# W2 issued behind W1 with a wait in the q/k queue, and fp16 chunk bounds for the second halves of the first batch

## The chip, the cores and the metric

The kernel runs on one core of one Trainium2 chip. The metric is the device time of one execution in microseconds (us). TensorE is called PE here, VectorE DVE, ScalarE ACT, GpSimd POOL and SyncE SP. SP issues most DMAs and computes nothing; POOL issues the loads of v, W1 and W2 and also computes.

## What is computed

Sparse attention over chunks of keys, followed by a layer norm and a two-layer MLP with a residual. There are 4 batches, 8 heads, 768 positions and 64 values per head, all fp32 in and out.

```python
k_min, k_max = min and max of k over each chunk of 32 keys      # 24 chunks
ub = sum_d max(q * k_min, q * k_max)                            # bound of each chunk
ub = where(chunk is not in the future, ub, -1e9)
top = the 6 chunks with the largest bound, for each query
scores = q @ k.T / 8, kept where the key's chunk is in top and the key is not in the future
x = softmax(scores) @ v, heads side by side                     # (4, 768, 512)
xn = (x - mean) / sqrt(var + 1e-6) * g_ln
out = x + relu(xn @ w_ch1) @ w_ch2                              # 512 -> 2048 -> 512
```

## The kernel before

A group is one batch and one pair of heads: 16 groups, four per batch. The 768 positions are six tiles of 128; a half is three tiles. Batch 0 (groups 0 to 3) is worked through by halves: first halves of all four groups, then the second halves. Its units are called (g, i), with i = 0 or 1. Groups 4 to 15 are worked through whole.

The steps of one unit, in the code's names:

- `load_qk`: four DMAs on SP's queue bring k and q of a half. `load_v`: v on POOL's queue, with a change of type to fp16.
- `turn`: PE transposes k or q (fp32) into PSUM.
- `k_bound`: DVE takes min and max over each chunk, into `kc`.
- `k_diag`: builds a block matrix `BD` from the bounds for both heads. For groups from 4 on, POOL also splits it into high and low fp16 parts in `BH`.
- `q_copy`: in batch 0 ACT makes fp32 relu(-q) and relu(q), `q32` and `r32`; from group 4 on it makes a high fp16 part of q, and DVE the low part; `q_relu` makes the same two for relu(q).
- `bounds`: PE computes the chunk bounds. In batch 0 one bf16 matmul writes the causal mask into PSUM and two fp32 matmuls per tile add the bounds; from group 4 on there are four fp16 matmuls per tile of 96 columns, high and low parts side by side.
- `select`: DVE finds the sixth largest bound with `max` and writes the mask `MN`. From group 4 on it first adds the two column parts and the causal mask, `causf`.
- `mask_t`, `mask_ring`: PE transposes the mask, DVE copies it beside q in the score tiles `QA` and `QB`. `k_copy` fills `KA` and `KB`; from group 4 on by DMAs on SP's queue.
- `scores`, `diag`, `values`, `normalise`: scores on PE, exp on ACT, the diagonal's mask on POOL, the product with v on PE, the division on DVE into x.
- `stats`, `centre`, `rstd`, `x_t`, `mlp1`, `mlp2`: the layer norm and the MLP of half a batch (b, r), all with fp16 weights. `mlp1` takes two blocks of 128 hidden columns at a time, W1 in four pieces; `mlp2(b, r, i, j)` takes four of the sixteen hidden blocks (kt 4j to 4j + 3) of output tile i, and W2 comes in four pieces j by the same kt. After the last, DVE scales, adds x and SP stores the tile.

The order is written out by hand. Every step is put into a list with a time (`at`, and the list `begin` for the start); `MOVED` shifts single steps; the list is sorted by time and then executed, each engine's instructions in that order, which for the start is also made fixed. PE, DVE, ACT and POOL each work through their queue in order, so a waiting instruction holds all behind it. The loads of the start stand in the table `loads`:

```python
        4: [(load_v, 1, 1), (load_v, 2, 1), (load_qk, 4, 0)],
        5: [(w2_load, 0, 0), (w2_load, 1, 0), (load_v, 3, 1), (load_qk, 4, 1)],
        6: [(w2_load, 2, 1), (w2_load, 3, 1)],
```

`w1_load` and `w2_load` first copy one element of a group's `kc` into the piece, on POOL: that makes the transfer wait until this group's `k_bound` is through. Both queues' DMAs are also limited in number: a DMA takes one of eight semaphores in turn and waits until the DMA that had it before has landed.

Of the kernel before, what the change touches and what calls it, by code (L numbers as in the profile page):

```python
# [9 lines left out]
ACTF = mybir.ActivationFunctionType  # L10
ALU = mybir.AluOpType
# [8 lines left out]
def kernel(  # L20
# [21 lines left out]
    NR = 2  # L42
# [44 lines left out]
    RT = const.tile([P, S], F16, name="RT", tag="RT")  # L87
    tiny = const.tile([1, 1], F32, name="tiny", tag="tiny")
# [75 lines left out]
    def w2_load(j, g):  # L164
        nc.gpsimd.tensor_copy(w2b[0:1, 4 * j, 0:1], st[g]["kc"][0:1, 0, NCH // 2:NCH // 2 + 1])
        nc.gpsimd.dma_start(w2b[:, 4 * j:4 * j + 4, :], w2_r[:, 4 * j:4 * j + 4, :])

# [59 lines left out]

    def q_copy(g, i):
        pst = st[g]["qn", i]
        if g < HP:  # L230
            u = P if i == 0 else 0
            for e, (nm, sign) in enumerate((("q32", -1.0), ("r32", 1.0))):
                st[g][nm] = prp.tile([P, TR * P], F32, name=nm, tag=nm)
                nc.scalar.activation(st[g][nm][:, u:], pst[:, u:], ACTF.Relu, scale=sign)
            c = cols(g, i)
            nc.scalar.activation(QA[g % NK][0:64, c], pst[0:64, :], ACTF.Copy, scale=QS)
            nc.scalar.activation(QB[g % NK][64:P, c], pst[64:P, :], ACTF.Copy, scale=QS)
            return
# [44 lines left out]
    def k_diag(g, i=None):  # L283
# [4 lines left out]
        e, eng = (0, nc.vector) if g < HP else (1, nc.gpsimd)  # L288
        if g >= HP:
            eng.tensor_tensor(kc[:, 1], kc[:, 1], kc[:, 0], ALU.subtract)  # L290
# [4 lines left out]
        if g >= HP:  # L295
            bh = BH[g % NB]
            nc.gpsimd.tensor_copy(bh[:, :, 0], bd)
            nc.gpsimd.tensor_tensor(bh[:, :, 1], bd, bh[:, :, 0], ALU.subtract)

    def bounds(g, s, i=None, idle=0):  # L300
        p = st[g]
        a, z, n = chosen(g, i)
        if g < HP:
# [16 lines left out]
        else:  # L320
# [3 lines left out]
            o = p["ub"][:, s - 1].rearrange("p l h c -> p (l h c)")  # L324
# [6 lines left out]
    def select(g, i=None):  # L331
# [4 lines left out]
        if g >= HP:  # L336
            ubt = smp.tile([P, NT - 1, 2, NCH], F32, name="ubt", tag="ubt", bufs=1)
            ubm = smp.tile([P, NT - 1, 2, NCH], F32, name="ubm", tag="ubm")
            nc.vector.tensor_tensor(ubt, ub[:, :, 1], causf, ALU.add)
            nc.vector.tensor_tensor(ubm, ub[:, :, 0], ubt, ALU.add)  # L340
            ub = ubm
# [176 lines left out]
    def mlp2(b, r, i, j):  # L518
# [4 lines left out]
        for kt in range(4 * j, 4 * j + 4):  # L523
            nc.tensor.matmul(  # L524
                yp, h["hT"][:, kt, i * P:(i + 1) * P], w2b[:, kt, :],
                start=(kt == 0), stop=(kt == KT2 - 1),
            )
        if j == 3:
            ot = outp.tile([P, DM], F32, name="ot", tag="ot")
            nc.vector.scalar_tensor_tensor(  # L530
                ot, yp, h["rstd"][:, i:i + 1], xh(b, r)[:, i].rearrange("p h d -> p (h d)"),
# [3 lines left out]
            nc.sync.dma_start(out[b, s * P:(s + 1) * P, :], ot)  # L535
# [11 lines left out]
        4: [(load_v, 1, 1), (load_v, 2, 1), (load_qk, 4, 0)],  # L547
        5: [(w2_load, 0, 0), (w2_load, 1, 0), (load_v, 3, 1), (load_qk, 4, 1)],
        6: [(w2_load, 2, 1), (w2_load, 3, 1)],
        8: [(load_v, 4), (load_qk, 5, 0)],  # L550
# [111 lines left out]
    for b in range(B):  # L662
# [14 lines left out]
        if b == 0:  # L677
# [13 lines left out]
            (): -0.04, (0, 1): -0.009, (0, 2): -0.025, (1,): 0.008, (1, 1): 0.017, (1, 2): 0.017,  # L691
            (2,): 0, (2, 4): 0.006, (2, 5): 0.028, (3,): 0, (3, 1): 0.013, (3, 2): 0.013,
            (4,): -0.048, (5,): 0.008, (5, 5): 0.016, (6,): 0.004, (7,): -0.067, (7, 1): -0.07,
            (8,): -0.436, (9,): -0.025, (9, 5): -0.02, (11,): -0.044, (12,): -0.311, (13,): -0.144,
            (14,): -0.138, (14, 5): -0.134, (15,): -0.21, (15, 4): -0.176, (15, 5): 0,
        },
        "centre": {
            (): 0.008, (0,): -0.017, (0, 1): 0, (0, 1, 0): -0.017, (1,): 0, (1, 0, 2): 0.089,
            (1, 1): 0.033, (1, 1, 1): 0.026,
        },  # L700
        "diag": {
            (): -0.046, (0, 0): 0.016, (0, 1): 0.001, (1, 0): 0.012, (1, 1): -0.067, (2,): 0.003,
            (3, 0): -0.003, (3, 1): 0, (4,): -0.056, (6, 0): -0.044, (6, 1): -0.066, (7, 0): -0.178,
            (7, 1): -0.097, (8, 0): -0.399, (8, 1): -0.6, (9, 0): -0.066, (9, 1): -0.069, (11, 0): 0,
            (11, 1): -0.054, (12, 0): -0.04, (12, 1): 0, (13, 0): -0.146, (13, 1): -0.078,
            (14, 0): 0.003, (14, 1): 0, (15, 0): -0.621,
        },
        "k_bound": {
            (0,): -0.011, (1,): -0.011, (2,): -0.009, (3,): -0.018, (4, 0): 0.007, (4, 1): 0.027,
            (5, 1): 0.022, (6, 0): 0.002, (6, 1): 0.107, (7,): -0.058, (8, 0): -0.331,  # L710
            (8, 1): -0.396, (9, 0): 0.002, (9, 1): 0.065, (11, 0): -0.008, (11, 1): 0.025,
            (12, 0): -0.017, (12, 1): -0.015, (13,): -0.032, (14,): 0.028,
        },
        "k_copy": {
            (0,): -0.004, (1, 0): 0.161, (1, 1): 0.063, (2,): 0.006, (3, 0): -0.011, (3, 1): 0.054,
            (4,): 0.024, (5, 0): 0.511, (5, 1): 0.42, (6,): 0.038, (7, 0): -0.032, (9, 1): 0.023,
            (10,): 0.034, (11, 1): 0.026, (12, 0): 0.938, (12, 1): 0.253, (13, 0): 0.002,
            (13, 1): 0.073, (14,): 0.046, (15,): 0.034,
        },
        "k_diag": {  # L720
            (1,): 0.041, (2, 0): 0.13, (3, 0): 0.033, (3, 1): 0.01, (4,): -0.002, (6,): 0.002,
            (7,): -0.058, (8,): -0.331, (9,): -0.138, (10,): -0.023, (11,): 0.02, (12,): 0.006,
            (13,): -0.032, (14,): -0.108, (15,): -0.076,
        },
        "load_qk": {
            (): -0.438, (0, 0): 0.085, (0, 1): -0.538, (1, 0): 0.034, (1, 1): -0.331, (2, 0): 0,
            (2, 1): -0.329, (3, 0): 0.16, (3, 1): -0.169, (4, 0): -0.33, (4, 1): -0.667,
            (5, 0): -0.543, (5, 1): -1.259, (6, 0): 0.011, (6, 1): -0.111, (7, 0): 0.064,
            (7, 1): 0.002, (8, 0): -0.299, (8, 1): -0.593, (10, 0): 0.015, (10, 1): -0.002,
            (11, 0): -0.01, (11, 1): -0.012, (12, 0): 0.082, (12, 1): 0.004, (13, 0): 0.11,  # L730
            (13, 1): 0.159, (14,): 0.026, (15, 0): 0.317, (15, 1): 0.334,
        },
        "load_v": {
            (2,): -0.087, (3, 0): -0.13, (3, 1): -0.568, (4,): -0.551, (5,): -0.547, (6,): -0.163,
            (7,): 0.215, (8,): -0.124, (9,): 0.342, (12,): 0.279, (13,): 0.241, (14,): 0.301,
            (15,): 0.238,
        },
        "mask_ring": {
            (): 0.017, (0, 0): 0.021, (0, 1): 0, (1, 0): 0.036, (1, 1): -0.009, (2, 0): 0.023,
            (2, 1): 0, (4,): 0.064, (5,): 0.074, (6,): 0.076, (7,): 0.016, (8,): -0.257, (9,): 0.076,  # L740
            (10,): 0.209, (11,): 0.066, (12,): 0.08, (13,): 0.102, (14,): 0.139, (15,): 0.093,
        },
        "mask_t": {
            (): -0.004, (0,): 0, (1, 0): -0.019, (1, 1): -0.002, (2,): 0.002, (4,): -0.016,
            (5,): -0.068, (7,): -0.064, (8,): -0.337, (10,): -0.001, (11,): -0.014, (12,): 0.002,
            (13,): -0.082, (14,): 0, (15,): -0.006,
# [144 lines left out]
```

## Time and profile before

| | |
|---|---|
| median of 3 runs | 302.92 us (302.92 to 303.49) |
| profiled execution | 303.4 us, span 301.4 us, PE clock granted 0.997 |
| DMA moved | 31.41 MB, mean 104 GB/s |
| MLP matmuls on PE, L512 and L524 | 94.3 and 95.9 us of records |
| exp on ACT, L417 | 86.2 us |
| `bounds` in fp32, L316 | 48 + 32 records in batch 0, 15.0 us |
| `bounds` in fp16, L326 | 240 matmuls, 23.1 us |

The span starts with the first instruction and ends with the last. Busy times of PE are sums of records that overlap, because matmuls are pipelined; the distance between starts tells what a matmul costs. An fp32 matmul leaves two records. Most of the DMA traffic falls in the first 80 us.

```profile
GB/s 131 208 210 198 180 199 196 164 193 204 149 135 187 124 72 165 110 143 148 88 132 62 78 46 2 41 49 90 35 37 0 37 37 35 35 37 35 70 37 71
```

Each number is one fortieth of the span, 7.5 us.

### The profile page before, as it was taken

The page shows a single profiled execution, that of the slowest core. Times are in us where ns is not written, and L with a number is a line of the kernel's source. Part 1 is how long each engine was busy: PE and PEld are TensorE (multiplying, and loading weights), DVE is VectorE, ACT ScalarE, POOL GpSimd, SP SyncE. Part 2 cuts the span into 40 slices and gives each one's busy share as a digit, 9 for nine tenths or more (in the row PEclk, how much of TensorE's full clock was granted, in tenths as well). Part 3 has the DMA queues.
Part 4 walks back from the last instruction along what each step waited for, and adds up shares of the span by engine and source line. Part 5 has one row for each costly group of instructions (what it writes and reads, how often), then busy time and mean ns, then how long its engine had stood idle before and what let it go on. Part 6 is the DMA issues. An engine that isn't in the chain of part 4 may idle for free.

```text
span 301.4 us, 7194 instructions
## 1 busy us (share of the span) xinstructions
PE 288.2 (96%) x2753; PEld 195.4 (65%) x2753; DVE 190.8 (63%) x654; ACT 183.5 (61%) x274; POOL 91.1 (30%) x162
## 2 busy tenths in 40 slices
PE   7887998999999999999999999999999999999993
PEld 3874766765777676777767667766666555555541
DVE  7888655679998788999577768577262282011011
ACT  3983997664788667778665674848368524423310
POOL 9559383152444412733230411223021120000000
PEclk9999999999999999999999999999999999999998
DMA  7999999999659649679572210113010110010111
GB/s 131 208 210 198 180 199 196 164 193 204 149 135 187 124 72 165 110 143 148 88 132 62 78 46 2 41 49 90 35 37 0 37 37 35 35 37 35 70 37 71
DMA packets 90226, 31.41 MB, mean 104 GB/s; under 512 B 78416, under 2 KB 87120, under 8 KB 90192
## 3 DMA queue, kind: packets, MB, share of 16 engines
q1 hardware_dynamic: 60416, 23.61, 33.8%
q0 software_dynamic: 29248, 7.34, 24.8%
q8 instruction: 22, 0.36, 0.5%
q14 instruction: 12, 0.10, 0.1%
q10 hardware_dynamic: 528, 0.00, 0.1%
HBM read 27.27 MB, written 6.29 MB: 111 GB/s over the span
## 4 chain that ended last, share of the span: by engine, by line
PE 75%; DMA 8%; POOL 7%; issue 4%; DVE 4%; ACT 1%; POOLq 0%; ACTq 0%
PE yp L524 24%; PE mm L512 24%; PE mm L411 10%; PE sm L437 6%; PE tr L223 4%; DMA w2b<-in_moe_w_ch_dram 4%; DMA w1b<-in_moe_w_ch_dram 4%; PE ub L326 3%; POOL va L214 2%; PE trh L497 1%; POOL pt L424 1%; PE trh L354 1%; DVE xc L482 1%; ACT pt L417 1%; POOL rstd L491 1%
## 5 line engine op out<-in xcount | busy, mean ns | idle before, releaser
L417 ACT ACTIVATE pt<-mm 128x1024 f16<-128x1024 f32 (+1 forms) x96 | 86.2, 918 | 25.7 <-PE mm L411 25.3
L524 PE MATMUL yp<-w2b,hT 128*128 128x512 f16 x384 | 95.9, 379 | 1.5 <-DMA w2b<-in_moe_w_ch_dram 1.5
L512 PE MATMUL mm<-xT,w1b 128*128 128x384 f16 x512 | 94.3, 326 | 0.0
L516 ACT ACTIVATE hT<-mm 128x768 f16<-128x768 f32 x64 | 51.9, 813 | 49.1 <-PE mm L512 48.8
L512 PEld LDWEIGHTS <-w1b 128*128 128x128 f16 x512 | 48.9, 98 | 29.9 <-issue 0.2
L524 PEld LDWEIGHTS <-hT 128*128 128x128 f16 x384 | 36.4, 98 | 31.8
L424 POOL TENSOR_SCALAR_AFFINE_SELECT pt<-pt 128x768 f16<-128x768 f16 x32 | 28.8, 899 | 89.1 <-ACT pt L417 89.1
L530 DVE SCALAR_TENSOR_TENSOR ot<-yp,rstd,x 128x512 f32<-128x512 f32 x24 | 17.9, 746 | 45.9 <-PE yp L524 45.9
L411 PE MATMUL mm<-QA,KA 128*128 128x128 f16 (+2 forms) x224 | 34.5, 245 | 1.0 <-ACT hT L516 0.5
L411 PE MATMUL mm<-QB,KB 128*128 128x128 f16 (+2 forms) x224 | 34.2, 246 | 0.0
L437 PEld LDWEIGHTS <-pt 128*128 128x128 f16 x672 | 24.6, 98 | 5.6 <-POOL pt L424 1.8
L437 PE MATMUL sm<-va,pt 128*128 128x65 f16 x672 | 26.5, 193 | 1.4 <-POOL pt L424 1.3
L411 PEld LDWEIGHTS <-KA 128*128 128x128 f16 x224 | 17.9, 99 | 8.1 <-issue 2.3
L471 DVE BATCH_NORM_STATS2 bst<-x 128x6 f32<-128x128 f32 x96 | 21.9, 282 | 0.8
L268 DVE TENSOR_REDUCE kc<-tr 128x12 f32<-128x384 f32 x32 | 17.6, 549 | 6.6 <-PE tr L223 4.9
L411 PEld LDWEIGHTS <-KB 128*128 128x128 f16 x224 | 18.0, 98 | 3.5 <-issue 0.8
L446 DVE RECIPROCAL rden<-sm 128x6 f32<-128x6 f32 x32 | 6.1, 191 | 19.7 <-PE sm L437 19.6
L447 DVE TENSOR_TENSOR x<-sm,rden 128x384 f32<-128x384 f32 x32 | 17.8, 557 | 1.0
L223 PE MATMUL tr<-ident_f,qn 128*128 128x128 f32 x96 | 16.2, 278 | 1.3 <-DMA qn<-in_q_dram 1.3
L269 DVE TENSOR_REDUCE kc<-tr 128x12 f32<-128x384 f32 x32 | 17.5, 547 | 0.0
L279 ACT CAST kh<-tr 128x384 f16<-128x384 f32 x24 | 11.6, 484 | 9.2 <-DMA KB<-kh 3.2
L223 PE MATMUL tr<-ident_f,kn 128*128 128x128 f32 x96 | 16.2, 278 | 0.0
(87 smaller groups left out, 354.2 us busy)
## 6 DMA issues: line engine op xcount, KB each, us to landing
kn<-in_k_dram SPq DMA_DIRECT2D x64, 96.0 KB, 3.3
qn<-in_q_dram SPq DMA_DIRECT2D x64, 96.0 KB, 3.7
out_dram<-ot SPq DMA_DIRECT2D x24, 256.0 KB, 2.1
va<-in_v_dram POOLq DMA_DIRECT2D x12, 192.0 KB, 5.5
w1b<-in_moe_w_ch_dram POOLq DMA_DIRECT2D x4, 512.0 KB, 7.7
w2b<-in_moe_w_ch_dram POOLq DMA_DIRECT2D x4, 512.0 KB, 11.2
KA<-kh SPq DMA_DIRECT2D x24, 48.0 KB, 2.1
KB<-kh SPq DMA_DIRECT2D x24, 48.0 KB, 2.0
```

Of the source, the lines that this page charges most:

```text
L223: nc.tensor.transpose(pst[:, t * P:(t + 1) * P], src[:, t], ident_f)
L268: nc.vector.tensor_reduce(kc[:, 0, n], view, axis=AX.X, op=ALU.min)
L411: nc.tensor.matmul(sc[:, hh, o:o + w * P], ks[:, t * P:(t + 1) * P], qs[:, s * P:(s + w) * P], start=True, stop=True,)
L417: nc.scalar.activation(pt[:, n0:n1].rearrange("p n h x -> p h n x"), sc[:, :, 0:o].rearrange("p h (n x) -> p h n x", x=P), ACTF.Exp, scale ...
L424: nc.gpsimd.affine_select(out=dv, in_=dv, compare_op=ALU.is_ge, fill=0.0, base=0, pattern=[[0, 2 * TR], [1, P]], channel_multiplier=-1,)
L437: nc.tensor.matmul(pv[:, hh, s2, :], pt[:, where[t, s], hh, :], va[:, hh, t, 0:D + 1], start=(t == 0), stop=(t == s),)
L447: nc.vector.tensor_tensor(xh(b, r)[:, :, 2 * hp:2 * hp + 2, :].rearrange("p s h d -> p h s d"), pv[:, :, :, 0:D], rden.to_broadcast([P, 2, ...
L471: nc.vector.bn_stats(h["st"][:, i, hp], xh(b, r)[:, i, 2 * hp:2 * hp + 2].rearrange("p h d -> p (h d)"),)
L512: nc.tensor.matmul(hp_[:, i, 0:TR * P], w1b[:, kt, (m + i) * P:(m + i + 1) * P], h["xT"][:, kt], start=(kt == 0), stop=(kt == KT1 - 1),)
L516: nc.scalar.activation(h["hT"][:, m:m + 2], hp_[:, :, 0:TR * P], ACTF.Relu, scale=HS)
L524: nc.tensor.matmul(yp, h["hT"][:, kt, i * P:(i + 1) * P], w2b[:, kt, :], start=(kt == 0), stop=(kt == KT2 - 1),)
L530: nc.vector.scalar_tensor_tensor(ot, yp, h["rstd"][:, i:i + 1], xh(b, r)[:, i].rearrange("p h d -> p (h d)"), op0=ALU.mult, op1=ALU.add,)
```

## The change

In batch 0's second halves the bounds are now computed as in the later groups: `whole(g, i)` is true for the first halves alone, and everything else takes the fp16 path with high and low parts. Unlike in the later groups, `k_diag` stays on DVE for them. W2's four loads are tied to group 3's bounds and stand between the v loads of batch 0's second halves. A new step, `after_w2`, puts a DMA of one element out of W2's last block on SP's queue, so that SP waits until this piece of W2 has landed. The very last output tile is computed in two column parts, 384 and 128, each with its own DVE operation and store. The shifts in `MOVED` are replaced for nearly all steps.

```diff
     def w2_load(j, g):
-        nc.gpsimd.tensor_copy(w2b[0:1, 4 * j, 0:1], st[g]["kc"][0:1, 0, NCH // 2:NCH // 2 + 1])
+        nc.gpsimd.tensor_copy(w2b[0:1, 4 * j, 0:1], st[g]["kc"][0:1, 0, 0:1])
         nc.gpsimd.dma_start(w2b[:, 4 * j:4 * j + 4, :], w2_r[:, 4 * j:4 * j + 4, :])
+    def after_w2():
+        nc.sync.dma_start(fence, w2b[0:1, KT2 - 1, 0:1])
...
+    def whole(g, i):
+        return g < HP and i == 0
...
     def q_copy(g, i):
         if g < HP:
-            u = P if i == 0 else 0
-            for e, (nm, sign) in enumerate((("q32", -1.0), ("r32", 1.0))):
-                st[g][nm] = prp.tile([P, TR * P], F32, name=nm, tag=nm)
-                nc.scalar.activation(st[g][nm][:, u:], pst[:, u:], ACTF.Relu, scale=sign)
+            if i == 0:
+                for nm, sign in (("q32", -1.0), ("r32", 1.0)):
+                    st[g][nm] = prp.tile([P, TR * P], F32, name=nm, tag=nm)
+                    nc.scalar.activation(st[g][nm][:, P:], pst[:, P:], ACTF.Relu, scale=sign)
+            else:
...
+                nc.scalar.activation(qh, pst, ACTF.Copy, scale=QS)
+                nc.vector.scalar_tensor_tensor(ql, pst, QS, qh, op0=ALU.mult, op1=ALU.subtract)
+                nc.vector.tensor_scalar_max(rh, qh, 0.0)
+                nc.vector.scalar_tensor_tensor(rl, qh, 0.0, ql, op0=ALU.is_gt, op1=ALU.mult)
...
     def k_diag(g, i=None):
-        e, eng = (0, nc.vector) if g < HP else (1, nc.gpsimd)
-        if g >= HP:
+        eng = nc.vector if g < HP else nc.gpsimd
+        e = 0 if whole(g, i) else 1
+        if e:
             eng.tensor_tensor(kc[:, 1], kc[:, 1], kc[:, 0], ALU.subtract)
...
-        if g >= HP:
+        if e:
             bh = BH[g % NB]
-            nc.gpsimd.tensor_copy(bh[:, :, 0], bd)
-            nc.gpsimd.tensor_tensor(bh[:, :, 1], bd, bh[:, :, 0], ALU.subtract)
+            eng.tensor_copy(bh[:, :, 0], bd)
+            eng.tensor_tensor(bh[:, :, 1], bd, bh[:, :, 0], ALU.subtract)
...
     def bounds(g, s, i=None, idle=0):
-        if g < HP:
+        if whole(g, i):
...
     def select(g, i=None):
-        if g >= HP:
+        if not whole(g, i):
...
     def mlp2(b, r, i, j):
-        for kt in range(4 * j, 4 * j + 4):
+        n, cs = 4, slice(0, DM)
+        if (b, r, i) == (B - 1, NR - 1, TR - 1):
+            n, cs = 8, slice(0, DM - P) if j < 2 else slice(DM - P, DM)
+        for kt in range(n * j % KT2, n * j % KT2 + n):
             nc.tensor.matmul(
-                yp, h["hT"][:, kt, i * P:(i + 1) * P], w2b[:, kt, :],
+                yp[:, cs], h["hT"][:, kt, i * P:(i + 1) * P], w2b[:, kt, cs],
                 start=(kt == 0), stop=(kt == KT2 - 1),
             )
...
-        4: [(load_v, 1, 1), (load_v, 2, 1), (load_qk, 4, 0)],
-        5: [(w2_load, 0, 0), (w2_load, 1, 0), (load_v, 3, 1), (load_qk, 4, 1)],
-        6: [(w2_load, 2, 1), (w2_load, 3, 1)],
-        8: [(load_v, 4), (load_qk, 5, 0)],
+        4: [(load_v, 1, 1), (w2_load, 0, 3), (w2_load, 1, 3), (load_qk, 4, 0)],
+        5: [(load_v, 2, 1), (w2_load, 2, 3), (w2_load, 3, 3), (load_v, 3, 1), (load_qk, 4, 1)],
+        8: [(load_v, 4), (after_w2,), (load_qk, 5, 0)],
```

In the built program, which the shifts decide, POOL's queue has after W1: v halves of groups 0 and 1, W2 pieces j = 0 and 1, v of group 2, W2 pieces j = 3 and 2, v of group 3. Before, it had the v halves of all four groups and then W2 j = 0, 1, 2, 3. `after_w2` stands behind 51 loads on SP's queue, ahead of the last load of the second half of group 6.

## The prediction

> **What bounds the kernel now.** I read the page first, then stretches of the span, then what TensorE (PE) waits for, then the timelines of POOL and PE around W2.
>
> ```profile
> PE 288.2 (96%) x2753; PEld 195.4 (65%) x2753; DVE 190.8 (63%) x654; ACT 183.5 (61%) x274; POOL 91.1 (30%) x162
> ```
>
> ```profile
> core 0: us, PE busy (x) PEld busy (x) DVE busy (x) ACT busy (x) POOL busy (x), PEclk, DMA share, GB/s
> 24.00:40.00 16.00, 15.00 (x110) 10.38 (x107) 11.20 (x43) 11.80 (x24) 10.33 (x16) 1.00 1.37 188
> 40.00:54.00 14.00, 12.06 (x123) 9.17 (x123) 7.88 (x24) 11.26 (x19) 7.03 (x13) 1.00 1.24 198
> 54.00:62.00 8.00, 8.00 (x90) 6.02 (x88) 5.86 (x19) 5.85 (x8) 2.76 (x6) 1.00 1.71 168
> 62.00:80.00 18.00, 17.42 (x201) 11.86 (x200) 15.69 (x56) 9.65 (x15) 7.34 (x13) 1.00 1.23 200
> 80.00:240.00 160.00, 159.60 (x1702) 112.69 (x1701) 115.97 (x397) 111.00 (x156) 45.49 (x80) 1.00 0.42 85
> ```
>
> From 54 us on PE stands still for about 1 us before its last matmul. So a microsecond of PE work removed anywhere, or of PE waiting added before 54 us, reaches the end nearly whole. Before 54 us PE has holes, and the largest is this one:
>
> ```profile
> 49.53 1.89 PE L524 MATMUL yp<-w2b,hT 128*128 128x512 f16 x8
> 52.96 0.38 PE L524 MATMUL yp<-w2b,hT 128*128 128x512 f16 x1 [1.54 <-DMA w2b<-in_moe_w_ch_dram]
> ```
>
> Eight matmuls use the first two W2 pieces; the ninth (kt 8) waits for piece j = 2. When do the pieces land? The POOL timeline:
>
> ```profile
> 36.02 0.77 POOL L214 DMA_DIRECT2D va<-in_v_dram  x1 [2.93 <-DMA w1b<-in_moe_w_ch_dram]
> ...
> 38.15 0.82 POOL L166 DMA_DIRECT2D w2b<-in_moe_w_ch_dram  x1 [0.30 <-POOL w2b L165]
> ...
> 40.66 0.75 POOL L166 DMA_DIRECT2D w2b<-in_moe_w_ch_dram  x1 [0.30 <-POOL w2b L165]
> ...
> 41.88 0.75 POOL L166 DMA_DIRECT2D w2b<-in_moe_w_ch_dram  x1 [0.30 <-POOL w2b L165]
> ```
>
> Asked one at a time, issue to landing is 8.1, 10.1, 12.3 and 14.3 us: they land at 46.2, 49.5, 52.9 and 56.2, one per 3.4 us. The last W1 piece lands at 25.14 + 10.6 = 35.7, the eighth v half at 36.02 + 6.3 = 42.3. So POOL's queue is never empty: 8 v halves in 6.5 us (0.82 each), then W2 at 13.9/4 = 3.48 each. Issue time does not matter, place in the queue does. Beside it q/k loads keep landing, at 45.8, 48.3, 50.8 and 53.4, every 2.5 us.
>
> **What the Trainium skill says.** "DMA: Bandwidth & Descriptors", section "Queues, rings and completion order": each DMA engine takes turns between the queues that have work. The trace agrees: 512 KB of W2 in 3.4 us beside a 96 KB q/k load every 2.5 us, for as long as both queues are full. "FP8 and Floating Point Precision", section "TensorE Precision Notes": true fp32 takes four passes through the array. The trace shows 0.22 us for an fp32 matmul of 48 columns, against 0.043 for fp16 of 96: more than four times.
>
> **The change part by part.**
>
> *Bounds of the four second halves of batch 0.* Removed on PE, per unit: a causal matmul and six fp32 ones, from 31.98 to 33.36, 1.38 us. Added: 12 fp16 matmuls of 96 columns; L326 x20 takes 0.85 us in the chain, so 0.51. Saved 0.87 x 4 = 3.5 us; the order of the built program has PE work otherwise unchanged. ACT: two relu of about 0.50 give way to one copy of 0.50, saving 2 us in all. DVE, added per unit: q low half 0.55 (L247), r high and low about 0.2 + 0.5 (L254 and L255 show 0.33 and 0.84 at 640 columns, here 384), three more small operations in k_diag about 0.2 + 0.2 + 0.3 (128x24 to 128x96, near L291's 0.31), two adds of 144 columns at 0.31 (L345's size). Together 2.6, 10 us for four. DVE's idle time from 24 to 54 is 4.8 + 6.1 = 10.9 us, so it just fits, but in one chain per unit: k reduce, k_diag, q parts, bounds, select, mask.
>
> Following that chain by hand in the new order: the first unit's high and low parts are ready near 31.3, the second's near 35.4; PE starts the first scores near 39.2 (40.21 before), waits for the second mask until about 42.8, and reaches the first W2 matmul near 49, against 46.9 if the 2.6 us saved by then counted whole. It reaches kt 8 near 50.7; bounds 49 and 53, an estimate from these rows.
>
> *W2.* Its pieces move ahead of four v halves, to the order v, v (group 0), v, v (group 1), W2 j = 0, 1, v, v (group 2), W2 j = 3, j = 2, v, v (group 3). POOL is still held by the same wait for the last W1 piece (36.02 above), now between the W2 pairs, but by then six transfers are queued. So kt 8's piece is now the last: behind it there are 6 v halves and 4 W2 pieces instead of 8 and 3. Landing: 35.7 + 6 x 0.82 + 4 x 3.48 = 54.6, against 52.9. Bounds: with the q/k queue silent W2 could take all of the 196 GB/s of that stretch, 2.7 us a piece, and v 0.25 to 0.5, so 49; with 0.95 us per v half, 55.5. I take 54.6, because the q/k queue holds about eight loads when it meets its new wait and hands out one per 2.5 us: it is not drained by then.
>
> *The wait in the q/k queue.* SP waits until the third W2 piece (j = 3) is in: 54.6 - 3.5 = 51.1. Behind it stand a q load of group 6, eight more loads, and the k copies into the score tiles of group 4 (KA, KB), which that group's scores wait for. Before, SP needed until 57.14 to reach those copies, because each load waits for an earlier one to land. Afterwards nine issues at 0.53 from 51.1 bring it to 56: no cost if the DMAs keep busy, at most about 2 us later for loads that PE uses beyond 66. The fence transfer is one element; I count it as nothing.
>
> *Last tile.* Its 16 matmuls of 512 columns become 16 of 384 and 16 of 128: 0.163 + 0.055 against 0.216, nothing. The last DVE operation shrinks from 0.75 to about 0.3 (128 of 512 columns; 0.42 is shown for 256), its store from 256 to 64 KB: 0.45 + 0.25 = 0.7 saved, between 0.4 and 1.0. Nothing hides it: it is the end.
>
> *Other moves.* Order beyond 62 us: PE events keep their places, all 3.5 us of PE work earlier; in the last 60 us part of batch 3's first MLP layer comes earlier. Since PE hardly waits there now, I count it at 0, bounds -0.5 and +1.
>
> *Sum*, against the profiled span of 301.4 (this execution: 303.4; the three timed runs 302.92 to 303.49). kt 8 starts at 54.6 instead of 52.96: +1.6. Of the 3.5 us, 2.6 lie before that wait and vanish in it; the fourth unit's 0.9 comes after: -0.9. End: -0.7. DVE has 0.6 more in the fourth unit's select just where it is busy 15.7 of 18 us: +0.3. Total +0.3: span 301.7, time 303.2.
>
> **The rivals.**
>
> *W2 arrives in time.* If the wait in the q/k queue empties it early, the pieces land at 2.7 us each and PE goes on at 50.7 to 52: -2.3 or -1, then -0.9 and -0.7: 299.0 to 300.4. For it: the wait is put there for this purpose, and 40 of the 196 GB/s are q/k. Against it: the eight loads already in the queue. Chance 0.25.
>
> *DVE becomes the bound (slower).* Its 10 us of new work sits in serial chains; it had 10.9 us idle before 54 and has 2.1 + 2.3 in 54 to 80. If more than about 4.4 us is outstanding when PE resumes, each further microsecond holds up bounds and masks of group 4 and so PE. At 6 to 7 outstanding: +2 on top of my sum, 305.2. For it: 62 to 80 is 87% DVE already. Against it: PE's W2 wait of some 4 us lets DVE catch up. Chance 0.22.
>
> *The change does not do what it says:* the wait only rearranges transfers, since the total to move is the same. That is my main case.
>
> **How the numbers follow.** About 0.2% (0.6 us) can be told from no change. Main case 0.53: its own range is 302.0 to 304.4, from W2's landing +-1 and the end +-0.3; of it 0.13 falls below 302.3, 0.20 within, 0.20 above 303.5. W2 in time: 0.25, faster. DVE bound: 0.22, slower. So faster 0.38, same 0.20, slower 0.42. The range that leaves about 1 in 10 out on each side runs from 300.2 to 305.3.
>
> **What would show it.** Right: PE's wait for w2b is about 4 us and ends near 54.6, with the fourth W2 piece landing last and eight L548 matmuls before it; 12 bounds matmuls in 0.51 us; the last DVE operation at 0.3 us; PE without holes afterwards. Wrong: a W2 wait under 2 us (the first rival); or PE waiting for DVE's masks and bounds for more than 2 us between 54 and 80 (the second). If neither wait is there and the time falls by 4 us, my reading of the DMA queues has failed.

## The result, and the profile after

The changed kernel takes 305.75 us in the median of four runs (305.21 to 305.86), the kernel before 303.17 (302.92 to 303.49). The ratio is 1.0081, with a 95% interval of 1.0064 to 1.0099: slower by 0.8%. The forecast was 303.2 us, with 300.2 to 305.3 as its range, so the result lies 0.45 us above the range's end. The profiled span grew from 301.4 to 303.5 us. Medians are those of all executions of a kernel; ratios and their intervals leave out the few that took clearly longer than the rest, such as one of 602 us in `w2_select_first`.

The first line of the page, as shown for before:

```profile
PE 287.9 (95%) x2765; PEld 193.2 (64%) x2765; DVE 201.1 (66%) x687; ACT 183.2 (60%) x270; POOL 90.8 (30%) x162
```

DVE has 10.3 us more work, as reckoned (10). PE's records cover about the same time, though 3.5 us of matmul work are gone: records overlap and take in small holes, so what PE loses has to be read from stretches and starts. The same stretches as before:

```profile
core 0: us, PE busy (x) PEld busy (x) DVE busy (x) ACT busy (x) POOL busy (x), PEclk, DMA share, GB/s
24.00:40.00 16.00, 13.65 (x107) 8.35 (x103) 13.90 (x48) 9.96 (x18) 12.16 (x20) 1.00 1.31 193
40.00:54.00 14.00, 11.35 (x115) 7.60 (x116) 12.56 (x48) 12.19 (x19) 2.30 (x5) 1.00 1.30 188
54.00:62.00 8.00, 7.44 (x88) 5.44 (x88) 6.34 (x21) 4.88 (x7) 2.42 (x6) 1.00 1.23 179
62.00:80.00 18.00, 17.66 (x204) 11.77 (x202) 16.14 (x52) 9.59 (x15) 9.19 (x17) 1.00 1.39 181
80.00:240.00 160.00, 158.75 (x1693) 112.32 (x1692) 118.22 (x402) 110.91 (x156) 46.76 (x80) 1.00 0.42 88
```

DVE went from 11.20 to 13.90 of 16 us and from 7.88 to 12.56 of 14. In its timeline it stands nowhere for more than 0.5 us between 35 and 54. PE, in turn, covers 1.35 and 0.71 us less of these two stretches, and 0.56 less of 54 to 62.

PE's timeline at W2, where before it waited 1.54 us until 52.96:

```profile
51.74 1.89 PE L548 MATMUL yp<-w2b,hT 128*128 128x512 f16 x8
54.33 0.81 PE L548 MATMUL yp<-w2b,hT 128*128 128x512 f16 x3 [0.69 <-DMA w2b<-in_moe_w_ch_dram]
```

kt 8 starts at 54.33, close to the 54.6 that I had reckoned for W2. But PE waits only 0.69 us: it came at 54.33 - 0.69 = 53.64, not at 50.7. The kernel before came at 52.96 - 1.54 = 51.42. So with 2.6 us less to do, PE was 2.2 us later.

POOL's timeline shows that the piece for kt 8 is the fourth issued; asked one at a time it landed at 54.29.

```profile
30.54 0.80 POOL L167 DMA_DIRECT2D w2b<-in_moe_w_ch_dram  x1 [0.30 <-POOL w2b L166]
...
31.84 0.75 POOL L167 DMA_DIRECT2D w2b<-in_moe_w_ch_dram  x1 [0.30 <-POOL w2b L166]
...
36.84 0.79 POOL L167 DMA_DIRECT2D w2b<-in_moe_w_ch_dram  x1 [0.30 <-POOL w2b L166]
...
38.10 0.75 POOL L167 DMA_DIRECT2D w2b<-in_moe_w_ch_dram  x1 [0.30 <-POOL w2b L166]
```

The end of the timeline, all engines:

```profile
298.52 0.62 DVE L554 SCALAR_TENSOR_TENSOR ot<-yp,rstd,x 128x384 f32<-128x384 f32 x1 [1.85 <-PE yp L548]
299.19 1.05 PE L548 MATMUL yp<-w2b,hT 128*128 128x128 f16 x16 [0.71 <-DVE ot L554]
...
300.28 0.35 DVE L554 SCALAR_TENSOR_TENSOR ot<-yp,rstd,x 128x128 f32<-128x128 f32 x1 [1.14 <-PE yp L548]
```

The last DVE operation is short, as meant. But the second column part's first matmul waits 0.71 us until DVE has read the first part: both parts lie in the same PSUM tile (that this is the reason is tested below).

From kt 8 to the end PE and its tail take 303.5 - 54.33 = 249.17 us, before 301.4 - 52.96 = 248.44. My sum had these 1.3 us shorter (-0.9 - 0.7 + 0.3); they are 0.7 longer. That is a miss of 2.0 us; kt 8 itself started 0.2 us sooner than reckoned (+1.4 instead of +1.6).

### The profile page after: what moved, and what is told of

Read it like the earlier page. It is cut to its first block, busy times and chain, and to the rows that moved or that the text cites. A ratio compares the mean times of both kernels' runs of the same rounds, so it can differ in the third digit from the quotient of the medians.

```text
span 303.5 us, 7263 instructions
## 1 busy us (share of the span) xinstructions
PE 287.9 (95%) x2765; PEld 193.2 (64%) x2765; DVE 201.1 (66%) x687; ACT 183.2 (60%) x270; POOL 90.8 (30%) x162
## 4 chain that ended last, share of the span: by engine, by line
PE 63%; DVE 13%; DMA 11%; POOL 6%; issue 4%; ACT 2%; SPq 1%; ACTq 0%; POOLq 0%
PE yp L548 24%; PE mm L532 20%; PE mm L431 7%; DMA w2b<-in_moe_w_ch_dram 5%; PE sm L457 5%; DMA w1b<-in_moe_w_ch_dram 3%; PE tr L228 3%; PE ub L345 2%; POOL va L219 2%; DVE kc L286 1%; DVE x L467 1%; DVE kc L287 1%; DVE r L273 1%; POOL pt L444 1%; DMA kn<-in_k_dram 1%
## 5 line engine op out<-in xcount | busy, mean ns | idle before, releaser
L437 ACT ACTIVATE pt<-mm 128x1024 f16<-128x1024 f32 (+2 forms) x96 | 86.2, 920 | 25.4 <-PE mm L431 24.9
L548 PE MATMUL yp<-w2b,hT 128*128 128x512 f16 (+2 forms) x400 | 95.6, 370 | 1.4 <-DVE ot L554 0.7
L548 PEld LDWEIGHTS <-hT 128*128 128x128 f16 x400 | 37.3, 98 | 33.1 <-issue 1.9
L554 DVE SCALAR_TENSOR_TENSOR ot<-yp,rstd,x 128x512 f32<-128x512 f32 (+2 forms) x25 | 18.2, 726 | 50.7 <-PE yp L548 50.7
L521 ACT ACTIVATE xT<-trh,gstr 128x384 f16<-128x384 f16 x16 | 9.1, 580 | 13.1 <-PE trh L517 13.0
L265 DVE SCALAR_TENSOR_TENSOR q<-tr,q 128x256 f16<-128x256 f32 (+1 forms) x24 | 11.6, 484 | 7.5 <-ACT q L264 7.3
```

Source lines behind the costliest of these rows:

```text
L437: nc.scalar.activation(pt[:, n0:n1].rearrange("p n h x -> p h n x"), sc[:, :, 0:o].rearrange("p h (n x) -> p h n x", x=P), ACTF.Exp, scale ...
L548: nc.tensor.matmul(yp[:, cs], h["hT"][:, kt, i * P:(i + 1) * P], w2b[:, kt, cs], start=(kt == 0), stop=(kt == KT2 - 1),)
```

## The experiments

Theory V: two chains meet at kt 8. DVE's new work delays PE's arrival to 53.6, W2's last piece holds it until 54.3; the saved matmuls are lost in both. Theory O: the new offsets in `MOVED` make the loss. Beside them stand my forecast's rivals: the wait in the q/k queue, and the column split. All ratios are to the kernel before, timed beside each run; the changed kernel's is 1.0081. The steps of the start get their times from their places in the list, so a kernel with other loads has some of its other steps shifted too: a run with other loads need not have quite the order of the one that it is compared with.

### One part at a time

`no_split`: the changed kernel with whole columns at the end.

```diff
-        if (b, r, i) == (B - 1, NR - 1, TR - 1):
+        if False:
```

> The changed kernel with the column split of the last output tile taken out, all else kept. In the trace of the changed kernel TensorE waits 0.71 us between the two column parts for VectorE's operation on the first. If the split gains 0.7 as I predicted: end 0.7 us later than the changed kernel, ratio to the kernel before about 1.0105. If the wait gives most of it back (the theory that I now hold): 0.2 to 0.4 us later, ratio about 1.009. If the wait eats more than the split saves: ratio 1.007 or lower. In none of the three does this alone explain the slowdown.

306.31 us, 1.0124 [1.0088, 1.0161]. The interval overlaps that of the changed kernel, so the time settles nothing. In the profiled execution, PE is 3.0 us late already at 26.57 (23.58 in the changed kernel). Nothing was edited there; the clock granted to PE was halved:

```profile
11.20:18.00 6.80, 6.80 (x42) 6.08 (x40) 4.09 (x17) 4.49 (x10) 1.27 (x3) 0.50 1.34 210
```

The third column from the right is that clock, PEclk. One other execution has the same mean clock over its span, 0.986, and took as long; the other four, at 0.997 and more, took 305.68 to 306.47. From kt 8 (57.40) to the end (306.7) it takes 249.3 us against 249.17: the split gives next to nothing in these two traces. The tail experiments below say why.

`order_before`: fp16 bounds, W2's place and the wait, with the old `MOVED` and no split.

> The changed kernel's fp16 bounds, W2 placement and wait, but every step at the offsets (table MOVED) of the kernel before, and no column split. If the fp16 bounds' VectorE chain is what costs (theory V): the first W2 matmul stays near 51 us or later and the time stays 1.005 to 1.012 of the kernel before. If the new order makes the small holes after 54 us (theory O): about 1.5 to 2 us better than the run without the split, ratio about 1.003.

308.76 us, 1.0191 [1.0163, 1.0219]. Far worse, not better: with the fp16 bounds, the old offsets are no cure. PE waits twice for long, the second time for a mask from DVE, and the first W2 matmul starts at 56.95. PE's timeline, then its windows:

```profile
44.65 0.45 PE L431 MATMUL mm<-QA,KA 128*128 128x128 f16 x2 [2.34 <-ACT pt L437]
...
56.77 0.34 PE L374 MATMUL trh<-ident_h,MN 128*128 128x128 f16 x3 [2.67 <-DVE MN L365]
```

```profile
44.85:48.20 3.35, 3.35 (x17) 2.07 (x15) 3.19 (x10) 2.17 (x3) 1.76 (x3) 0.50 1.43 177
48.30:54.00 5.70, 5.23 (x73) 4.06 (x71) 2.59 (x8) 5.17 (x10) 0.62 (x2) 1.00 1.26 192
54.00:60.00 6.00, 3.33 (x26) 2.15 (x26) 3.91 (x18) 3.04 (x4) 1.38 (x2) 1.00 1.69 139
```

Behind the first wait the clock is halved, behind the longer second one it is not.

`fp16_only`: the kernel before with only the fp16 bounds (old offsets, old W2 loads, no wait, no split).

> The kernel before with only the fp16 bounds of the second halves: W2 as before, no wait in the q/k queue, the order of before, no column split. Theory V: VectorE is busy without a gap from 29 to 54 us, TensorE reaches kt 8 no earlier than 53.5 although W2's piece j = 2 lands at 52.9, and the time is 1.003 to 1.01 of before. Rival (W2's new place and the wait cost the time): 3.5 us of TensorE work gone, TensorE waits for W2 at 52.9 as before and then saves 0.9, ratio 0.997.

309.3 us, 1.0197 [1.017, 1.0224]. So the fp16 bounds in the old order cost 6 us, even more than theory V said. W2's piece j = 2 landed at 52.60 as before, and PE took kt 8 without a wait in a run that starts at 54.51. The other part of the loss is one I had not thought of. PE's timeline of `fp16_only`, then its windows:

```profile
44.75 0.58 PE L431 MATMUL mm<-QA,KA 128*128 128x128 f16 x2 [2.34 <-ACT pt L437]
```

```profile
42.00:45.00 3.00, 0.66 (x6) 0.44 (x5) 2.87 (x14) 2.94 (x6) 1.73 (x4) 0.72 1.22 201
45.00:48.00 3.00, 3.00 (x15) 1.88 (x13) 2.83 (x8) 2.12 (x3) 1.67 (x3) 0.50 1.22 196
48.00:51.00 3.00, 3.00 (x17) 1.89 (x16) 1.31 (x5) 1.66 (x3) 0.00 (x0) 0.64 1.24 201
```

PEclk falls to 0.50: around a hole of 2.34 us the clock granted to PE is halved, PE works at it for some 5 us, and matmuls of 384 columns start every 0.320 us instead of 0.163. "PE busy" reads 3.00 of 3.00 there. The halved stretch by itself:

```profile
43.32:50.13 6.81, 5.38 (x22) 3.31 (x22) 5.76 (x21) 4.59 (x7) 2.08 (x4) 0.50 1.22 198
```

The Trainium skill has it in "TensorE: Matmul & The Clock Gate", section "What's actually happening": the clock gate passes half the pulses after an idle window of about 3.4 us, and the windows run freely, whatever the kernel does. The length agrees: 6.8 us is two such windows, and the 3.4 us in `order_before` is one. The hole that the page asks for does not: the clock was halved 0.9 us after the hole began (42.41), with a hole of 1.52 us (39.36 to 40.88) ahead of it, so PE was never idle for 3.4 us. Behind a wait of 1.96 us for a mask, until 66.09, the clock is halved once more, for 3.4 us from 67.2. The changed kernel's order keeps its holes between 24 and 54 us at 1.05 us and less, and its clock at 1.00.

`w2_only`: the kernel before with only W2's place and the wait.

> The kernel before with only W2's earlier place and the wait in the q/k queue: fp32 bounds, order and last tile of before. By my sum of the DMA queues the piece j = 2 now lands at 54.3 to 54.6 if it is issued last (in this order of steps it may be issued third, then near 51): TensorE's wait for it goes from 1.54 us to about 3 us or to about 0. Theory V: nothing else changes, ratio 0.995 with the piece third, 1.005 with it last. Rival (the wait in the q/k queue starves group 4's loads): holes of 1 us or more between 56 and 70 us and a ratio over 1.008.

303.2 us, 1.0001 [0.9981, 1.0021]: no difference. In the order that comes of the other loads PE issues the first four W2 matmuls at 51.38, other work, and the next eight at 56.29 and 58.51; the third piece has landed at 52.57 and the fourth at 55.89. The W2 wait is gone and the time is not. PE's timeline, then DVE's:

```profile
51.20 0.34 PE L359 MATMUL trh<-ident_h,MN 128*128 128x128 f16 x3 [1.59 <-DVE MN L350]
```

```profile
48.76 0.20 DVE L451 RECIPROCAL rden<-sm 128x6 f32<-128x6 f32 x1 [0.19 <-PE sm L442]
48.99 0.56 DVE L452 TENSOR_TENSOR x<-sm,rden 128x384 f32<-128x384 f32 x1
49.59 0.68 DVE L476 BATCH_NORM_STATS2 bst<-x 128x6 f32<-128x128 f32 x3
50.18 0.62 DVE L349 MAX8 m<-ub 128x8 f32<-128x24 f32 x6
```

A wait of 1.59 us for a mask has taken its place. DVE finds that mask (L349) only after the first unit's normalisation and statistics, although its bounds were done before 48. While W2 was late, this cost nothing.

### What makes PE late at kt 8

`no_low_halves`: the changed kernel, with the operations for `ql` and `rl` of batch 0 left out. PE issues as many matmuls, with the high parts in their place; these bounds lack the low part of q.

```diff
-                nc.vector.scalar_tensor_tensor(ql, pst, QS, qh, op0=ALU.mult, op1=ALU.subtract)
                 nc.vector.tensor_scalar_max(rh, qh, 0.0)
-                nc.vector.scalar_tensor_tensor(rl, qh, 0.0, ql, op0=ALU.is_gt, op1=ALU.mult)
```

> The changed kernel without the two VectorE operations that make the low halves of q and r for the second halves of batch 0 (0.55 us each, four units: 4.4 us). TensorE issues the same matmuls, with the high halves in the place of the low ones, so the bounds there lack the low part of q. Theory V (VectorE's chain before 54 us sets TensorE's pace): TensorE stands before kt 8 some 1.5 to 3 us earlier, near 51 to 52, then waits for W2 until 54.3 as now (wait 2 to 3.5 us instead of 0.69), and only small holes after it vanish: ratio to the kernel before 1.002 to 1.006. Theory O (the new order makes the loss): arrival and ratio unchanged, 1.008.

307.14 us, 1.0119 [1.0084, 1.0154]. PE's timeline, then the windows:

```profile
55.11 1.01 PE L546 MATMUL yp<-w2b,hT 128*128 128x512 f16 x2 [4.08 <-DMA w2b<-in_moe_w_ch_dram]
```

```profile
54.00:57.00 3.00, 1.89 (x9) 1.16 (x9) 0.51 (x2) 0.00 (x0) 0.00 (x0) 0.64 1.80 203
57.00:60.00 3.00, 3.00 (x24) 2.14 (x23) 1.43 (x4) 2.16 (x3) 0.00 (x0) 0.79 0.68 143
```

PE comes at 55.11 - 4.08 = 51.03: taking 4.4 us of work from DVE brings PE 2.6 us forward. That part of theory V holds, and so does W2's landing. The time was missed: W2's piece, landing at 55.06 here, turns the earlier arrival into one long hole, and the clock is lower behind it, 0.64 and 0.79 in the mean of these two stretches. A faster DVE makes this kernel no faster.

`k_diag_on_pool`: k_diag's operations for those units on POOL.

```diff
-        eng = nc.vector if g < HP else nc.gpsimd
+        eng = nc.vector if whole(g, i) else nc.gpsimd
```

> The changed kernel with the four small k_diag operations of each second half of batch 0 moved from VectorE to GpSimd: about 0.9 us of VectorE work less per unit, 3.6 in all. Theory V: if GpSimd is free, TensorE reaches kt 8 about 1 to 2 us earlier, ratio 1.004 to 1.007. But GpSimd stands 3 us and more at its DMA issues near 33 to 37 us and its operations take longer, so that bounds may come later than now: then 1.010 to 1.015. Theory O: 1.008.

305.47 us, 1.007 [1.0038, 1.0103]. PE waits 1.45 us and goes on at 54.39: it comes at 52.94, 0.7 us sooner, and gets nothing for it. W2 is the later chain by a little, as theory V has it.

`w2_in_order`: pieces issued 0, 1, 2, 3.

```diff
-        5: [(load_v, 2, 1), (w2_load, 2, 3), (w2_load, 3, 3), (load_v, 3, 1), (load_qk, 4, 1)],
+        5: [(load_v, 2, 1), (w2_load, 3, 3), (w2_load, 2, 3), (load_v, 3, 1), (load_qk, 4, 1)],
...
-            (1,): -0.002, (3,): -0.034,
+            (1,): -0.002, (2,): -0.034,
```

(`after_w2` reads the block of the third piece issued, as before.)

> The changed kernel with W2's pieces issued 0, 1, 2, 3 instead of 0, 1, 3, 2, the queue's wait still on the third issued. The piece for kt 8 lands 3.4 us earlier, near 50.9, so kt 8 starts when TensorE gets there. If TensorE's arrival at 53.64 is set by VectorE (theory V), the gain is the 0.69 us wait and no more: ratio 1.0055 to 1.007. If W2's landing had held TensorE back by more than the trace shows (my first reckoning, arrival at 50.7), kt 8 starts near 51 and the ratio is 0.997 to 1.000.

305.15 us, 1.0071 [1.0048, 1.0093]. PE takes kt 0 to 10 in one run from 51.41, without a wait. The later holes lie 0.9 to 1.0 us sooner against the span's start, 0.3 of which this execution had gained before 24 us. The interval overlaps that of the changed kernel, so this rests on the traces: some 0.7 us is what W2's order costs, and not more. PE's arrival is DVE's doing.

`no_low_w2_in_order`: both together.

> The kernel without the low halves of q (bounds of batch 0's second halves lack the low part of q), and W2's pieces issued 0, 1, 2, 3. Without the low halves TensorE came to kt 8 at 50.9 and waited 4.1 us, after which its granted clock fell to 0.64 between 54 and 57 us. If VectorE's chain set the arrival and the long hole the clock: now kt 8 starts near 51.6, the hole is under 1 us, the clock stays at 1.00, and the time falls 4 us or more below the run with W2 out of order: ratio to the kernel before 0.995 to 1.000. If leaving out the low halves costs in some other way: hardly any gain, 1.010.

304.29 us, 1.0057 [1.0033, 1.0081]. kt 8 starts at 51.95, the clock stays at 1.00, and the profiled span is 3.2 us shorter than that of `no_low_halves`. The two chains are told apart: less work on DVE alone gains nothing, W2 in order alone some 0.7 us, both together 2.4 us at kt 8. But the ratio stays above my 1.000: of these 2.4 us, 1.5 are left at the end. A hole of 1.07 us behind ScalarE at 100 us took part of it back.

`fp32_new_order` and `fp32_w2_in_order`: everything of the change but the fp16 bounds, first with W2's pieces 0, 1, 3, 2 and then in order.

> Everything of the change but the fp16 bounds: W2's place, the wait in the q/k queue, the new offsets and the column split, with the fp32 bounds of the kernel before. Theory V: VectorE has its gaps again, and the time is that of the kernel before less the split's gain, ratio 0.997 to 1.001. Theory O: the new offsets, made for the fp16 bounds or not, keep the holes after 54 us: ratio 1.004 or more.

> The fp32 bounds of the kernel before with W2's place, the wait in the queue, the new offsets and the column split, and W2's pieces issued 0, 1, 2, 3. With the pieces 0, 1, 3, 2 TensorE stood 4 us before kt 8 and then ran at half clock until 61: 1.0169. If that hole made all of the loss: kt 8 starts near 51.8, clock 1.00, about 5 us less, ratio 0.998 to 1.002. If the new offsets themselves do not suit the fp32 bounds: ratio over 1.006.

308.22 us, 1.0169 [1.0129, 1.0208], and 304.05 us, 1.0041 [1.002, 1.0061]. PE's timeline and windows of the first, then the same windows of the second:

```profile
55.31 0.38 PE L533 MATMUL yp<-w2b,hT 128*128 128x512 f16 x1 [3.81 <-DMA w2b<-in_moe_w_ch_dram]
```

```profile
54.00:62.00 8.00, 6.69 (x34) 5.08 (x34) 2.24 (x5) 2.62 (x4) 0.00 (x0) 0.65 1.03 155
```

```profile
54.00:62.00 8.00, 7.89 (x86) 5.27 (x85) 5.88 (x20) 5.59 (x8) 3.84 (x9) 1.00 1.01 155
```

The piece out of order costs 4 us here, a hole of 3.81 us and a mean clock of 0.65 in the 8 us stretch. With it mended the new offsets still do not suit the fp32 bounds. So theory O has a share; `late_order_before` looks for it.

### The queue's wait, the later offsets, the tail

`no_queue_wait`: `(after_w2,)` taken out of the table of loads.

> The changed kernel without the wait for W2 in the q/k queue, all else kept. By my sum of the queues the q/k loads take turns with W2 either way: the pieces land at most 1 us later (kt 8 at 54.3 to 55.3) and the loads of groups 5 and 6 some us earlier. If the wait costs later (the q load for which TensorE stands 0.5 us near 87): that hole goes, ratio 1.006. If it does what it is for: pieces 1 to 3 us later, W2 wait 2 to 3.5 us, ratio 1.011 or more. If nothing: 1.008.

306.6 us, 1.0119 [1.0099, 1.014]. In the trace W2's four pieces take 11.1, 13.1, 13.8 and 15.8 us from issue to landing; in the changed kernel, with the wait, 11.8, 13.9, 14.1 and 16.2. From the landing of the last W1 piece to that of kt 8's piece it is 18.99 us in both (36.59 to 55.58, 35.30 to 54.29). So the wait does not bring W2 in sooner, although SP stands in it for 5.3 us; the holes at 87 and 88 us are there with or without it, later by the 1.4 us that this execution is late. The time went up all the same. In the profiled execution the granted clock was 0.50 from 7.8 to 14.6 us, and PE was 2.1 us later than in the changed kernel by 25.65, before the step that was taken out. The two executions with a mean clock of 0.988 took 307.20 and 307.48; the other three took 305.60, 306.15 and 306.60, against 305.21 to 305.86 of the changed kernel. So a part of the 0.4% is the clock at the start; three executions are too few to say whether the edit has a part in the rest.

`late_order_before`: the old offsets from group 6 and batch 1 on.

> The changed kernel, but from group 6 and batch 1 on every step has the offset of the kernel before. After 62 us the changed kernel's TensorE has about 1.5 us more of small holes than before (at 87.4, 88.5, 124.8 and 147.0). Theory O: these belong to the new offsets; with the old ones they go, and the time falls by 1 to 1.6 us, ratio 1.003 to 1.005. If they follow from what comes before 62 us (loads or VectorE running late): still there, ratio 1.007 to 1.009.

305.66 us, 1.0101 [1.0074, 1.0128]. From kt 8 (54.00) to the second column part (298.66) PE takes 244.66 us; the changed kernel, 54.33 to 299.19, 244.86. So these offsets are worth 0.2 us, not 1.5: the holes at 124.8 and 147.0 went and others came. This leaves the offsets of groups 4 and 5 and of batch 0's MLP.

That offsets make the later holes can be read from the other traces. I take each distance between the starts of two matmuls, less the distance that the first one's size needs, and add up what is left between 80 and 240 us. With the old offsets this is 2.1 us, with fp32 bounds (the kernel before and `w2_only`) and with fp16 bounds (`order_before` and `fp16_only`, in the same work, which they reach 6 to 7 us later). With the new offsets it is 3.7 us in the changed kernel and 3.9 in `fp32_w2_in_order`; with the new ones up to group 5 alone, here, 3.4. The holes of 0.51, 0.34 and 0.54 us at 87.4, 88.5 and 147.0 recur, within 0.01 us, in `w2_in_order` and `fp32_w2_in_order`, and are not in the kernel before or in `w2_only`. So beyond 80 us the holes come with the new offsets and not with the fp16 bounds, and mostly with those of groups 4 and 5 and batch 0's MLP.

`after_own_tile` and `before_own_tile`: the split, its second part in a PSUM tile of its own, in the changed kernel and in the kernel before (there with one offset, -0.009, for that tile's steps).

```diff
             n, cs = 8, slice(0, DM - P) if j < 2 else slice(DM - P, DM)
+            if j == 2:
+                h["yp"] = yp = ps_t.tile([P, DM], F32, name="yp", tag="one")
```

> The changed kernel with the second column part of the last tile in a PSUM tile of its own. If the 0.71 us wait between the parts comes of the shared tile: TensorE goes straight on, the span is 0.7 to 0.9 us shorter, ratio 1.005 to 1.0065. If the wait has another cause (the weights, the clock): 1.008 as the changed kernel.

> The kernel before with only the column split of the last output tile, its second part in a PSUM tile of its own. By my sum: the last VectorE operation 0.75 to 0.35 us and the store 3.78 to 2.87 us as the changed kernel shows them, less about 0.2 for 32 narrower matmuls: 1.1 us sooner, ratio 0.996 to 0.9975. If the second store queues behind the first: 0.4 us or less, ratio 0.9985 to 1.

305.17 us, 1.0056 [1.0033, 1.0078], and 302.31 us, 0.9971 [0.9949, 0.9992]. The second is faster than the kernel before, by the 1.1 us that were reckoned: its span is 300.1 instead of 301.4, of which 0.2 had been gained by kt 8 already. In both PE goes straight on: the wait of 0.71 us came of the shared tile. Without it the split is worth 1.1 us, with it 0.4.

`after_two_mended`: W2 in order and the own tile, in the changed kernel.

> The changed kernel with W2's pieces issued 0, 1, 2, 3 and the second column part of the last tile in a PSUM tile of its own. If the two losses are separate, 0.7 and 0.9 us go: span near 301.8, ratio 1.002 to 1.005, still not faster than before, because the fp16 bounds' VectorE chain (arrival at kt 8 at 53.6) is left. If VectorE's chain costs nothing beside them: 0.998.

304.29 us, 1.003 [1.0016, 1.0044]. The two losses add, within the noise, and what is left of the change is still slower than the kernel before: the fp16 bounds and the new offsets.

### A kernel better than both

`w2_select_first`: `w2_only`, with the mask's selection ahead of normalisation and statistics.

```diff
         "select": {
-            (1, 1): 0.01, (2, 0): -0.003, (2, 1): 0.002, (3, 0): -0.004, (3, 1): 0.048, (4,): 0.059,
+            (1, 1): 0.01, (2, 0): -0.003, (2, 1): -0.1, (3, 0): -0.004, (3, 1): 0.048, (4,): 0.059,
```

> The kernel before with W2's earlier place and the wait in the queue, and VectorE's selection for the third unit of second halves put ahead of the normalisation and the statistics of the first. With W2 early alone, TensorE stood 1.59 us at 49.6 to 51.2 for that selection's mask, and the time was unchanged (1.0001). If the freed W2 wait had been turned into this mask wait: the mask's transposes start near 49.6, kt 8's piece is in by then, and the whole 1.6 us reaches the end: ratio 0.993 to 0.996. If W2's next piece or the ScalarE chain holds TensorE at once: 0.998 to 1.001.

303.07 us, 0.9977 [0.9954, 0.9999]. PE's timeline:

```profile
49.57 0.33 PE L359 MATMUL trh<-ident_h,MN 128*128 128x128 f16 x3
49.74 1.03 PE L529 MATMUL yp<-w2b,hT 128*128 128x512 f16 x4
```

The mask is there when PE comes, 1.63 us sooner than in `w2_only`. That the wait for W2 had been turned into the wait for the mask is shown. The profiled span is 299.6, 1.3 us shorter than in `w2_only`, but its executions, without the one of 602 us, are spread from 301.4 to 304.1, so less is gained in the median.

`w2_select_own`: with the split and its own tile besides. `w2_select_own_kh4`: with four buffers for `kh` as well.

```diff
-        kh = smp.tile([P, TR * P], F16, name="kh", tag="kh")
+        kh = smp.tile([P, TR * P], F16, name="kh", tag="kh", bufs=4)
```

> The kernel before with W2's earlier place and queue wait, the third unit's selection ahead of normalisation, and the column split with a PSUM tile of its own; fp32 bounds and the other offsets as before. If both parts add: 1.6 and 1.1 us, ratio 0.990 to 0.993, better than both kernels. If the selection gives nothing: 0.996 to 0.998.

> w2_select_own with four buffers for kh, the fp16 copy of k that DMAs carry into KA and KB, instead of two. If the wait for those DMAs makes the slower executions of w2_select_own (301.1 to 304.0): ScalarE's 1.42 us wait is gone, the executions draw together near 301.3, ratio 0.992 to 0.995. If the loads as such come late: no change, 0.997.

302.43 us, 0.997 [0.9952, 0.9988], spread from 301.1 to 304.0 in 22 executions; and 300.92 us, 0.9921 [0.9892, 0.995], all six within 300.56 to 301.27. The first is no better than `before_own_tile` (0.9971): in the median, the earlier mask gives nothing there. In its profiled execution, ScalarE shows a wait that can make the spread:

```profile
96.25 0.48 ACT L284 CAST kh<-tr 128x384 f16<-128x384 f32 x1 [1.42 <-DMA KB<-kh]
```

It cannot write the next k until a DMA has emptied one of two buffers, and PE stood 1.07 us for the exp behind it. With four buffers the same instruction of the second starts without a wait, and the spread is gone. The holes between 80 and 240 us, reckoned as above, fall from 4.1 to 2.1 us. Four buffers in the kernel before, without the rest, were not tried. This kernel is 2.3 us faster than the one before and 4.8 faster than the changed one. It keeps the fp32 bounds.

## Why the prediction was wrong

It said no change (303.2) as the likeliest, and slower with 0.42. The step that failed is the one on the order after kt 8, *other moves*, counted at 0. By the prediction's own steps:

- *W2's landing* (54.6): right, 54.29. The reading of POOL's queue as a sequence holds, and so does that the wait in the q/k queue only rearranges transfers: the landing was not sooner with it.
- *PE's arrival at kt 8* (50.7, bounds 49 and 53): wrong, 53.64. I had followed the chain per unit and let each unit start when its input was there. DVE takes its operations in the order written and had hardly any idle time left; what it does for one unit stands in front of the mask of another. 51.03 is what came out with 4.4 us of its work taken away. At kt 8 this error cost nothing, because W2's piece landed later still; that the sum had this start nearly right (+1.6, measured +1.37) is owed to W2. But the 3.5 us could not have been had with W2 in time either: `w2_in_order` shows it.
- *"Of the 3.5 us, 2.6 lie before that wait and vanish in it; the fourth unit's 0.9 comes after"*: the first half is borne out by the start of kt 8; the 0.87 of the fourth unit I take as reckoned.
- *The tail* (-0.7): the mechanism was right and the size wrong. From the end of the last matmul to the end of the span it went from 4.56 (296.84 to 301.4) to 3.26 us (300.24 to 303.5), better than reckoned. But I costed the matmuls at nothing; they take 0.2 more, and the wait for the shared tile is 0.71. Net -0.4.
- *DVE's knock-on* (+0.3) and *other moves* (0, bounds -0.5 and +1). What is left of 249.17 - 248.44 = +0.73, after -0.87 for the fourth unit and -0.4 for the tail, is +2.0. PE's small holes, reckoned from starts as above, add up to 3.6 us before and 5.6 after, from kt 8 to the last tile: +0.4 up to 80 us, where PE waits for an exp and for a mask, and +1.6 from 80 to 240. The first is near the +0.3. The second is the failing step, "Since PE hardly waits there now, I count it at 0": it comes with the new offsets, mostly those of groups 4 and 5 and of batch 0's MLP. Which of these shifts makes which hole is open. My ground for the 0 was weak too: the "about 1 us" for which PE stands still after 54 was read from busy times, whose records cover small holes; by starts it is 3.6.

The sum of these terms, +1.37 - 0.87 - 0.4 + 2.0 = +2.1, is the difference of the spans; the last is what the others leave, and the count of the holes confirms it.

Of the rivals, *W2 in time* is out. *DVE becomes the bound* came nearest, on the right side and at 305.2, but by luck, for its place was wrong: DVE was nearly full from 24 to 54 (26.5 of 30 us), not from 54 to 80, where PE's waits for it sum to 0.7 us at most. My test for it, over 2 us of such waits after 54, would have called it false. *The change does not do what it says*, my main case, is right for the wait in the queue, and its price fell short because the order after 80 us was counted at nothing. None of my cases had the clock in it; in the changed kernel it did not matter, but in six of the profiled runs it made a part of the loss.

## What to carry to other kernels

When a wait is to be taken away, look for the next one behind it on the same engine: here the mask, then the buffers of `kh`. With W2 early and the mask moved little reached the median; with the buffers and the split's own tile as well, 2.3 us did. Work moved to an engine with as much idle time as the work is long does not fit, if the idle time is made of waits in a chain. Where a tile is split so that two engines overlap, give the parts separate buffers.

## What the hardware showed that was not expected

Until PE's last matmul the clock granted to it was either 1.00 or 0.50, and it stood at 0.50 for 3.4 or 6.8 us at a time; the values between in the windows above are means over parts of both. It was halved around or behind holes of 1.96, 2.34 (two runs), 3.81 and 4.08 us, so a long hole on PE can cost more than its length. Length alone does not decide it. It stayed at 1.00 behind holes of 1.45 to 1.59 us in `before`, `w2_only` and `k_diag_on_pool`, and also behind the 2.67 us in `order_before`. If the windows of 3.4 us are counted on from the end of the halved stretch there (48.24), one ends near 55.1, within that hole (54.10 to 56.77), so that neither window was idle for more than about half of its length; that would explain it, but it is an estimate that no run tests. And in `no_split` and `no_queue_wait` it was halved near the start, though no hole before it, but for the span's first 1.35 us, was longer than 0.98 us; why is open.

An order that divides one long wait into several short ones can therefore be worth more than the sum of its waits shows. The changed kernel's offsets do so for its fp16 bounds: 1.0191 with the old ones (`order_before`), 1.0081 with the new ones and the split. Of the 3.3 us between these two spans, the 3.4 us at half the clock are some 1.7, by estimate.
